# A weight load moved from behind the first norm of an attention stage to behind its key cast

## The chip, the cores and the metric

The kernel runs on one core of one Trainium2 chip. The metric is the device time of one execution in microseconds (us). PE is the matrix engine, PEld its weight loads, DVE the vector engine, ACT the scalar engine, POOL the GpSimd engine and SP the SyncE engine, which here only issues DMAs. DMAs are issued by SP (hardware queue, q1 in the profile) and by POOL (software queue, q0), and both queues are served by the core's 16 DMA engines.

## The reference

Inputs are q, k, v of shape (8 batches, 8 heads, 576 tokens, 64), two spectral weights `w_r` and `w_i` of 64 modes x 512 x 512, and `w_ch` of 512 x 512, all fp32. First comes causal attention in a window of 128 tokens with a linear distance bias per head, then a Fourier mixing layer on its output.

```python
scores = scale * q @ k.T;  rel = i - j
scores = where((rel >= 0) & (rel < 128), scores - slope[h] * abs(rel), -1e9)
x = softmax(scores) @ v                     # heads side by side: (8, 576, 512)
X = rfft(x, axis=1)[:, :64]                 # 64 modes
Yr = Xr @ w_r - Xi @ w_i;  Yi = Xr @ w_i + Xi @ w_r      # one 512x512 matrix per mode
u = x + irfft(Y, n=576, axis=1)
out = u + relu(u @ w_ch)
```

The 128 matrices of `w_r` and `w_i` are 1 MB each in fp32. They are the bulk of what has to be read.

## The kernel before

**Attention.** The work is cut into 16 units, one for each batch and half of the heads (four heads). A unit has a fixed list of steps: three casts from fp32 to bf16 on DVE (`cast` of q and k at L241, of v at L236 and L238), transposes of q and k on PE with an evacuation each (L253, L259), four score tiles (`score`, L287), four exponentials on ACT (`exp`, L297), two multiplications by the decay table (`mask`, L308), two value products (`value`, L334), and two norms (`norm`: a reciprocal at L349 and a multiplication at L350 that writes x). At the end of each second unit come the forward Fourier products (`spectrum`, L371) and their evacuation (`channels`, L392).

**The order of the work** is written out by hand. `STAGE` (L38 to L44) lists the steps of one pipeline stage with a lag for each; the loop at L544 runs the list once for each stage, and a step of lag l works on unit `stage - l`. So the key cast (lag -2) of a stage is that of unit `stage + 2`, the query cast (lag -3) that of unit `stage + 3`, and the two norms (lag 1) are those of unit `stage - 1`. On DVE the order within a stage is: cast of v, cast of k, first norm, cast of q, the two masks, second norm. Each engine executes its instructions in the order in which they are written; engines wait for each other by semaphores.

**Loads of q, k and v.** Each cast issues, on SP, the load of the unit two further on into the buffer that it has just read (L243): one DMA of 576 KB for q or k, and five for v (four of 128 KB, one of 64 KB). There are two buffers for each of q, k and v. SP issues them in order, and each of its DMAs also waits for the DMA eight before it on SP.

**Weights.** `load_w` (L453) issues one weight matrix on POOL: 1 MB of fp32 is read and 512 KB of bf16 is written, cast on the way. One tile is issued ahead of the loop (L516), one in each of the stages 1 to 13 (`AHEAD`, L418) into the pool `early`, and seven more (`LATER`, L419) at the ends of stages 12 to 15 into q, k and v buffers that are no longer needed. So that the weight of a stage is not issued at once, POOL first copies one element that the first norm of the stage has written (L556):

```python
if stage in AHEAD:
    if stage:
        b, g = at.units[stage - 1]
        nc.gpsimd.tensor_copy(gate[:1, :1], x[:1, b, 0, 256 * g : 256 * g + 1])
    load_w(AHEAD[stage], early)
```

The copy has no other use. POOL does nothing else in these stages, so it stands at the copy until the norm is done and then issues the weight.

**After attention.** The other weights follow in the order of use, into pools whose buffers come free when attention ends and later when PE has used an earlier tile (`load_packs`, L465, two matrices at a time). PE multiplies the spectra of all batches by each matrix (L861). Between these products come inverse Fourier products, the projection by `w_ch` and the transposes that they need. After the last matrix the last four modes are patched in, and the output is computed and stored (L784 to L830).

Of the kernel before, what the change touches and what calls it, by code (L numbers as in the profile page):

```python
# [71 lines left out]
def _forward_table(nc, pool, F, S):  # L72


    NM = F.shape[2] // 2
    tok = pool.tile([P, FULL + 1], I32)
    nc.gpsimd.iota(tok[:, :FULL], [[P, FULL]], base=0, channel_multiplier=1)
    for bb in range(2):
        nc.gpsimd.iota(
            tok[64 * bb : 64 * bb + 64, FULL : FULL + 1], [[0, 1]],  # L80
            base=FULL * P, channel_multiplier=1,
        )
    mode = pool.tile([P, NM], I32)
    nc.gpsimd.iota(mode, [[1, NM]], base=0, channel_multiplier=0)
    prod = pool.tile([P, FULL + 1, NM], FP32)
    nc.vector.tensor_tensor(
        out=prod,
        in0=tok.unsqueeze(-1).broadcast_to([P, FULL + 1, NM]),
        in1=mode.unsqueeze(1).broadcast_to([P, FULL + 1, NM]),
        op=ALU.mult,  # L90
    )
    turn = pool.tile([P, FULL + 1, NM, 2], FP32)
    for ri in range(2):
        nc.vector.tensor_scalar(turn[:, :, :, ri], prod, float(S) / (4 - 2 * ri), 1.0 / S,
                                op0=ALU.add, op1=ALU.mult)
    whole = pool.tile([P, FULL + 1, NM, 2], FP32)
    nc.vector.tensor_scalar(whole, turn, MAGIC, MAGIC, op0=ALU.add, op1=ALU.subtract)
    nc.vector.tensor_tensor(out=turn, in0=turn, in1=whole, op=ALU.subtract)
    nc.scalar.activation(F[:, : FULL + 1].rearrange("p a b -> p (a b)"),
                         turn.rearrange("p a b c -> p (a b c)"), AF.Sin, scale=TWO_PI)  # L100
    yield
    nc.gpsimd.memset(F[:64, FULL + 1], 0.0)
    nc.gpsimd.tensor_copy(F[64:, FULL + 1], F[64:, FULL])
    nc.gpsimd.memset(F[64:, FULL], 0.0)
# [298 lines left out]
def kernel(  # L403
# [10 lines left out]
    nc = tc.nc  # L414
# [9 lines left out]
    x = const.tile([P, B, FULL + 1, DM], BF16, name="x")  # L424
# [4 lines left out]
    gate = const.tile([P, 8], BF16, name="gate")  # L429
# [23 lines left out]
    def load_w(n, pool, chosen=None):  # L453

        for i in ([i for i in todo_w if i not in again][:n] if chosen is None else chosen):
            todo_w.remove(i)
            src = (moe_w_r, moe_w_i)[i % 2][i // 2].rearrange("(p a) e -> p a e", a=4)
            homes[i] = pool
            t = spare.pop(0) if pool is None else pool.tile([P, 4, DM], BF16, tag="w", name="w")
            for part in ((slice(0, 4),) if i < 2 * NM - 1  # L460
                         else (slice(0, 2), slice(2, 3), slice(3, 4))):
                nc.gpsimd.dma_start(out=t[:, part], in_=src[:, part])
            wq[i] = [t[:, a] for a in range(4)]
# [27 lines left out]
    with ExitStack() as actx:  # L491
        at = _Attention(tc, actx, q, k, v, (ident, F, FT), x, XC, raw)
        n = len(at.units)
        for w, u in (("q", 0), ("k", 0), ("q", 1), ("k", 1), ("v", 0), ("v", 1)):
            at.load(w, u)
        done = set()

        def run(name, arg, u):
            if 0 <= u < n and (name, arg, u) not in done:
                done.add((name, arg, u))  # L500
                getattr(at, name)(u, arg)

        make_identity(nc, ident)
        pool = _Scratch(x[:, B - 2 :].rearrange("p b t c -> p (b t c)").bitcast(FP32))
        wt = at.ps.tile([P, P], FP32, tag="av", bufs=1, name="warm")
        for _ in range(24):
            nc.tensor.matmul(wt, lhsT=ident, rhs=ident, start=True, stop=True)
        table = _forward_table(nc, pool, F, S)
        next(table)
        nc.vector.memset(norm, 2.0 / S)  # L510
        nc.vector.memset(norm[:32], 1.0 / S)
        for t in at.qkT:
            nc.vector.memset(t[:, 1, :, S:], 0.0)
        at.distances(pool)
        at.fixtures(0)
        load_w(1, early)  # L516
        next(table, None)
        at.fixtures(1)
        nc.gpsimd.memset(XC[:, 4 * NC * NM :], 0.0)
        run("cast", "q", 0)  # L520
        run("transpose", "q", 0)
        run("cast", "k", 0)
        run("transpose", "k", 0)
        run("evacuate", "q", 0)
        for h in (1, 3):
            at.decay(h)
        run("evacuate", "k", 0)
        run("score", 1, 0)
        for h in (0, 2, 1, 3):
            at.offset(h)  # L530
        run("cast", "q", 1)
        run("transpose", "q", 1)
        run("evacuate", "q", 1)
        run("score", 0, 0)
        run("exp", 1, 0)
        for h in (0, 2):
            at.decay(h)
        run("exp", 0, 0)
        run("cast", "k", 1)
        run("cast", "v", 0)  # L540
        side = {0: [(at.offset, 4), (at.offset, 6), (at.decay, 5), (at.offset, 5), (at.decay, 7),
                    (at.offset, 7), (at.decay, 4), (at.decay, 6)]}
        lags = [lag for _, _, lag in STAGE]
        for stage in range(min(lags), n + max(lags)):  # L544
            for name, arg, lag in STAGE:
                run(name, arg, stage - lag)
                if name in ("transpose", "exp") and side.get(stage):
                    for _ in range(1 + (name == "transpose")):
                        fn, h = side[stage].pop(0)
                        fn(h)  # L550
            if stage == 3:
                at.inverse_table()
            if stage in AHEAD:
                if stage:
                    b, g = at.units[stage - 1]
                    nc.gpsimd.tensor_copy(gate[:1, :1], x[:1, b, 0, 256 * g : 256 * g + 1])  # L556
                load_w(AHEAD[stage], early)
            if stage in LATER:
                load_w(LATER[stage], None)

    with ExitStack() as mctx:
# [273 lines left out]
        for g in range(NM // 4):  # L835
# [5 lines left out]
            for i in range(8):  # L841
                k = 8 * g + i
# [159 lines left out]
```

## Time and profile before

| | us |
|---|---|
| median of 3 runs | 439.54 |
| lowest, highest | 439.48, 439.64 |
| span of the profiled execution | 439.4 |
| first and last gate copy (L556) start | 28.0, 118.3 |
| last attention exponential on ACT ends | 133.1 |
| weight products of PE (L861) | 140.8 to 405.7 |

| engine | busy us | share of the span |
|---|---|---|
| PE | 320.6 | 73% |
| DVE | 183.7 | 42% |
| ACT | 162.1 | 37% |
| POOL | 87.0 | 20% |

The profile is one execution, taken by the hardware profiler; its span runs from the first instruction to the last. The shares of busy time are means over parts that have different limits: attention up to about 140 us, the stream of weights up to about 405 us, and the output. In the rows of a timeline, the first number is the start, the second the duration (for several instructions from the first start to the last end), and the brackets give the idle time of the engine before it and what ended that. In a table of stretches the DMA share is the mean busy share of the 16 DMA engines; packets of two queues on one engine can overlap in the records, so that it goes somewhat over 1. GB/s counts bytes as written, so a weight counts with its 512 KB of bf16.

### The profile page before, as it was taken

What the parts mean: (1) busy time and instruction counts of PE and PEld (TensorE: products, weight loads), DVE (VectorE), ACT (ScalarE), POOL (GpSimd) and SP (SyncE); (2) the same over time, 40 slices, a digit from 0 to 9 for tenths busy, and PEclk for the clock granted to TensorE, in tenths of its full rate; (3) what the DMA queues carried; (4) which work ended last, traced back from release to release, by engine and by line L of the source; (5) the groups of instructions that cost most, each with busy time, mean ns of one, the idle gap of its engine ahead of it and who ended that gap; (6) DMA issues with size and microseconds to landing.
All of it is one profiled execution on the core that took longest, in us unless ns stands there. A gap on an engine that the chain in (4) does not pass through costs nothing. (4 is left out here: it accounts for less than half of the span.)

```text
span 439.4 us, 8314 instructions
## 1 busy us (share of the span) xinstructions
PE 320.6 (73%) x3509; PEld 177.6 (40%) x3509; DVE 183.7 (42%) x332; ACT 162.1 (37%) x211; POOL 87.0 (20%) x162
## 2 busy tenths in 40 slices
PE   4679899969796724553443387999889999698982
PEld 3357577647665411111111133444444444233430
DVE  7689699788783301010000022332222232122684
ACT  6769799987781000000000012323232323101780
POOL 8611011100323101322113111111111110012500
PEclk8679899999999965555555569999999999989997
DMA  8999999999999999999999999999999999997598
GB/s 280 306 329 301 300 292 312 266 302 283 266 224 213 216 214 213 214 213 214 214 213 215 214 214 214 214 215 215 214 214 215 216 213 214 214 215 135 199 368 306
DMA packets 52489, 105.54 MB, mean 240 GB/s; under 512 B 4052, under 2 KB 23396, under 8 KB 52452
## 3 DMA queue, kind: packets, MB, share of 16 engines
q0 software_dynamic: 18992, 67.22, 76.5%
q1 hardware_dynamic: 33460, 37.79, 26.3%
q8 instruction: 27, 0.44, 0.4%
q14 instruction: 10, 0.08, 0.0%
HBM read 162.53 MB, written 9.44 MB: 391 GB/s over the span
## 5 line engine op out<-in xcount | busy, mean ns | idle before, releaser
L861 PE MATMUL acc<-w,XC 128*32 128x512 bf16 x456 | 80.8, 485 | 68.8 <-DMA w<-in_moe_w_i_dram 35.4
L861 PEld LDWEIGHTS <-XC 128*32 128x32 bf16 x508 | 38.7, 148 | 110.1 <-issue 85.0
L297 ACT ACTIVATE att<-sc 128x1024 bf16<-128x1024 f32 x64 | 64.0, 1031 | 10.0 <-PE sc L287 10.0
L627 ACT CAST ZW<-zw 128x512 bf16<-128x512 f32 x8 | 4.7, 586 | 144.7 <-PE zw L625 144.7
L334 PE MATMUL av<-vb,att 128*128 128x132 bf16 (+1 forms) x576 | 38.4, 217 | 11.6 <-DVE x L350 8.8
L599 DVE TENSOR_SCALAR yq<-acc 128x512 bf16<-128x512 f32 x14 | 9.6, 687 | 82.2 <-PE acc L861 82.2
L334 PEld LDWEIGHTS <-att 128*128 128x128 bf16 x704 | 36.6, 98 | 17.2 <-DVE x L350 13.0
L693 PE MATMUL my<-wch,xT 128*64 128x512 bf16 x288 | 34.5, 381 | 5.8 <-ACT x L724 4.3
L702 ACT CAST XW<-my 128x512 bf16<-128x512 f32 x36 | 19.3, 589 | 50.5 <-PE my L650 50.5
L674 DVE COPY xT<-tr 128x1024 bf16<-128x1024 bf16 x18 | 12.5, 692 | 55.0 <-PE tr L672 55.0
L259 ACT COPY qkT<-tp 128x1152 bf16<-128x1152 bf16 x30 | 33.5, 1115 | 5.3 <-PE tp L253 4.5
L481 POOL DMA_DIRECT2D w<-in_moe_w_i_dram x23 | 16.3, 710 | 66.9 <-PE acc L861 44.2
L481 POOL DMA_DIRECT2D w<-in_moe_w_r_dram x22 | 15.6, 709 | 68.5 <-PE acc L861 48.1
L287 PE MATMUL sc<-qkT 64*64 64x256 bf16 (+2 forms) x640 | 25.7, 269 | 2.5 <-ACT qkT L259 1.6
L350 DVE TENSOR_TENSOR x<-av,rec 128x640 bf16<-128x640 f32 x32 | 26.4, 825 | 1.1
L693 PEld LDWEIGHTS <-xT 128*64 128x64 bf16 x288 | 17.1, 109 | 21.6 <-issue 9.2
L817 DVE TENSOR_TENSOR o<-yy,r 128x1024 f32<-128x1024 f32 (+1 forms) x22 | 21.5, 1025 | 4.8 <-DMA Z<-yq 2.6
L236 DVE CAST vb<-vr 64x1024 bf16<-64x1024 f32 x32 | 22.7, 708 | 0.4 <-DMA vr<-in_v_dram 0.2
L287 PEld LDWEIGHTS <-qkT 64*64 64x64 bf16 x640 | 14.8, 110 | 19.8 <-issue 16.5
L556 POOL COPY gate<-x 1x1 bf16<-1x1 bf16 x13 | 5.5, 423 | 86.2 <-DVE x L350 86.2
L724 ACT CAST x<-my 128x512 bf16<-128x512 f32 x18 | 10.6, 586 | 31.0 <-PE my L650 31.0
L274 PE MATMUL sc<-bias,ident 128*128 128x512 bf16 x64 | 20.7, 408 | 1.1 <-ACT att L297 1.1
(134 smaller groups left out, 431.0 us busy)
## 6 DMA issues: line engine op xcount, KB each, us to landing
w<-in_moe_w_i_dram POOLq DMA_DIRECT2D x23, 1024.0 KB, 35.8
w<-in_moe_w_r_dram POOLq DMA_DIRECT2D x22, 1024.0 KB, 35.7
qr<-in_q_dram SPq DMA_DIRECT2D x16, 576.0 KB, 9.2
kr<-in_k_dram SPq DMA_DIRECT2D x16, 576.0 KB, 8.2
vr<-in_v_dram SPq DMA_DIRECT2D x64, 128.0 KB, 7.6
w<-in_moe_w_r_dram POOLq DMA_DIRECT2D x16, 512.0 KB, 14.3
w<-in_moe_w_i_dram POOLq DMA_DIRECT2D x13, 512.0 KB, 24.0
out_dram<-o SPq DMA_DIRECT2D x13, 512.0 KB, 4.6
```

The costliest lines, as they stand in the source:

```text
L236: nc.vector.tensor_copy(self.vb[u % 2][row, :, :, :, W * half : W * half + D], src[row, :2])
L259: (self.nc.vector.tensor_copy if u < 2 and w == "q" else self.nc.scalar.copy)(dst.rearrange("q h (p j) -> q h p j", j=TPP), tp.rearrange(" ...
L274: nc.tensor.matmul(sc[:, e], lhsT=self.ident, rhs=self.bias[:, hv].rearrange("p j n -> p (j n)"), start=True, stop=False, skip_group_check ...
L287: nc.tensor.matmul(sc[64 * half : 64 * half + 64, e, j * 256 + c0 : j * 256 + c0 + n], lhsT=qkT[row, 1, h, k0 + j : k0 + P : 2], rhs=qkT[r ...
L297: self.nc.scalar.activation(self.att[u % 2][:, kt * 8 * P : (kt + 1) * 8 * P], sc.rearrange("p e n -> p (e n)"), AF.Exp, scale=1.0 / math. ...
L334: nc.tensor.matmul(bank[:, qt * W : qt * W + rhs[j].shape[1]], lhsT=att[:, o : o + P], rhs=rhs[j], start=(n == 0 and j == 0), stop=(n == l ...
L350: nc.vector.tensor_tensor(out=self.x[:, b, :, cs].rearrange("p t (h d) -> p h t d", h=2), in0=tiles[:, :, :, :D], in1=rec.unsqueeze(-1).br ...
L481: nc.gpsimd.dma_start(out=t.rearrange("p s a e -> p s (a e)"), in_=w[kinds.pop()][m : m + 2].rearrange("m (p a) e -> p m (a e)", a=4))
L693: nc.tensor.matmul(mm[ROWS[half]], lhsT=lhsT, rhs=wch[:, dt], start=(dt == 0), stop=False, skip_group_check=True,)
L702: nc.scalar.copy(XW[:, j, n], mms[n])
L817: nc.vector.tensor_tensor(out=o[:, c], in0=yy[:, c], in1=r[:, c], op=ALU.add)
L861: nc.tensor.matmul(into[32 * (m % 4) : 32 * (m % 4) + 32], lhsT=XC[:, c0 : c0 + 31 * NM + 1 : NM], rhs=wq[t][a], start=(ri == 0 and a == 0 ...
```

## The change

The element that POOL copies ahead of the weight of a stage is no longer one of x, written by the first norm of unit `stage - 1`, but one of the bf16 key tile, written by the key cast of unit `stage + 2` in the same stage. On DVE that cast stands just ahead of the first norm.

```diff
             if stage in AHEAD:
-                if stage:
-                    b, g = at.units[stage - 1]
-                    nc.gpsimd.tensor_copy(gate[:1, :1], x[:1, b, 0, 256 * g : 256 * g + 1])
+                nc.gpsimd.tensor_copy(gate[:1, :1], at.casted[stage + 2, "k"][:1, 0, 0, :1])
                 load_w(AHEAD[stage], early)
```

The order of the instructions is the same on each engine. The copies are 13 before and 13 after. As POOL now reads the key tile, of which there are two, the key cast that writes the same buffer two stages later waits for POOL too (eleven casts); three casts into x of the later part (L725) no longer wait for POOL.

## The prediction

> **What bounds the kernel now.** I read the page's 40 slices first, then the chain of work that ended last, then stretches of one attention stage each, then the GpSimd (POOL) timeline and the waits of the DMA-issuing queues.
>
> The slices and the queue table of the page:
>
> ```profile
> PE   4679899969796724553443387999889999698982
> ACT  6769799987781000000000012323232323101780
> DMA  8999999999999999999999999999999999997598
> ...
> q0 software_dynamic: 18992, 67.22, 76.5%
> q1 hardware_dynamic: 33460, 37.79, 26.3%
> ```
>
> The DMA engines are full from the second slice (11 us) to about 400 us, while PE and ACT have long empty stretches in between. The two queues together are worth 102.8% of 16 engines over the span. Queue 0 carries the weights (issued by POOL, cast on the way), queue 1 the loads of q, k, v and the output.
>
> The end of the PE timeline, where the last weights are used (start, duration, line, count, and the idle time before):
>
> ```profile
> 397.80 1.02 PE L861 MATMUL pa<-w,XC 128*32 128x512 bf16 x4 [0.58 <-DMA w<-in_moe_w_r_dram]
> 400.24 1.02 PE L861 MATMUL pa<-w,XC 128*32 128x512 bf16 x4 [0.22 <-DMA w<-in_moe_w_i_dram]
> 405.27 0.38 PE L861 MATMUL acc<-w,XC 128*32 128x512 bf16 x1 [0.19 <-DMA w<-in_moe_w_i_dram]
> ```
>
> PE waits for the last pieces of weight, so 405.3 us is set by the weight stream. The chain of the page covers only what follows (from 406.3 us), and that tail of 439.4 - 405.3 = 34.1 us has no weight load in it. So the time is the end of the weight stream plus a fixed tail, and an edit in the attention stages counts only by what it does to that stream.
>
> Now the stages. Stretches from one weight issue to the next; the columns are length, busy time (instructions) of PE, PEld, DVE, ACT and POOL, then granted clock, DMA share, GB/s:
>
> ```profile
> 59.30:66.50 7.20, 6.81 (x126) 5.11 (x126) 6.59 (x13) 6.70 (x8) 1.16 (x4) 1.00 1.02 278
> 79.50:86.70 7.20, 6.34 (x114) 5.13 (x112) 6.48 (x12) 6.47 (x9) 0.89 (x2) 1.00 1.05 292
> 118.70:130.40 11.70, 10.79 (x198) 8.42 (x196) 9.24 (x18) 9.91 (x12) 3.73 (x9) 1.00 1.10 238
> 130.40:140.00 9.60, 6.46 (x120) 5.17 (x118) 4.87 (x11) 3.25 (x6) 4.60 (x8) 1.00 1.06 213
> ```
>
> PE, DVE and ACT are at about nine tenths in a stage, and yet the DMA share is at or above 1.02 in every one of the 15 stretches that I asked for between 21 and 140 us. The last stretch is weights alone (213 GB/s). From about 122 us on, the stream does not break before 400 us: rates of 213 to 216 GB/s in nearly all later slices.
>
> **The change, step by step.** It removes 13 one-element POOL copies that read the first norm's output and puts 13 in their place that read the key cast of the same stage; nothing else moves in any engine's order. The weight DMA is the next instruction on POOL, so what moves is its issue.
>
> 1. How far. The POOL and DVE timelines of one stage:
>
> ```profile
> 77.21 0.76 DVE L241 CAST k<-kr 128x1152 bf16<-128x1152 f32 x1
> 77.88 0.21 DVE L349 RECIPROCAL rec<-av 128x10 f32<-128x10 f32 x1
> 78.13 0.82 DVE L350 TENSOR_TENSOR x<-av,rec 128x640 bf16<-128x640 f32 x1
> ...
> 79.09 0.18 POOL L556 COPY gate<-x 1x1 bf16<-1x1 bf16 x1 [6.12 <-DVE x L350]
> 79.54 0.71 POOL L462 DMA_DIRECT2D w<-in_moe_w_r_dram  x1 [0.27 <-issue]
> ```
>
> The key cast ends at 77.97, the norm at 78.95. The issue moves forward by 1.0 to 1.1 us (reciprocal 0.21 plus multiply 0.82 plus gaps). In one stage the norm waits 1.49 us for PE, and there it is 2.6 us (cast end 47.58, gate 50.29). Where the gate copy took 0.57 rather than 0.18 us, it ran beside the query cast; it would now run beside the norm, so up to 0.4 us more may come. I take 1.1 to 1.5 us in twelve stages and some 3 us in one.
>
> 2. What that does to the stream. Each tile is 512 KB, 524,288 B / 214 GB/s = 2.45 us of all DMA engines, now and after. No byte is added, none goes. With the engines full, an earlier start puts a weight in front of loads that then finish later by the same engine time; the end of all the work stays. Term: 0 us, exact only as far as the engines are full. How far they are not, bounds the term. In 1 us slices between 20 and 121 us the DMA share is under 1.00 in twelve; the deficits add up to 0.52 us, the largest a slice at 0.76 (61 to 62 us). A second way: q and k of a unit are 1.18 MB at the 393 GB/s of the slices 26 to 28 us, 3.0 us; v is 0.59 MB at the 306 GB/s of 28.5 to 31 us (1100 of its 1205 packets are under 2 KB), 1.9 us; with the weight, 7.4 us per stage. The gates lie (118.3 - 28.0) / 12 = 7.5 us apart, so 12 x 0.12 = 1.5 us is the most that better packing could save. I take -0.1 us, close to nothing, because the dips lie on both sides of a weight transfer, and a shift fills one and opens another.
>
> 3. What the moved weight displaces. Twelve of the stages have loads of v, k and q under way. Their consumers: DVE waited 7.4 us in all for q (6 times, longest 2.1), 0.3 for k, 0.2 for v. A later q lengthens that stage's compute, but compute is not the bound there: the next stages' loads are already queued. Term: 0; without that cover, up to 1.1 us once, not per stage, since the shift is the same in each stage.
>
> 4. The end of attention. After 118.7 us, weights are queued back to back; five single tiles (2.45 us each) are issued by 123.5 us, and POOL then waits:
>
> ```profile
> 123.47 0.54 POOL L462 DMA_DIRECT2D vr<-in_moe_w_i_dram  x1 [2.64 <-DMA vr<-in_v_dram]
> 129.35 1.06 POOL L462 DMA_DIRECT2D vr<-in_moe_w_r_dram  x2 [5.34 <-DVE vb L236]
> ```
>
> The pair at 129.35 waits for the last v cast. Its tiles land 9.0 and more (median 10.3) us after issue; the quickest landing of a tile in the stages was 6.6 us. So about 3.7 us pass before a late pair leaves the DMA engines empty. The last v load lands within the 0.6 us after 127.4 us (4 packets of queue 1 there, none later), and its cast runs at 128.97: 1.5 us of slack ahead of that. The last v load may be 5 us later before the stream breaks. Term: 0.
>
> 5. The new waits. Eleven key casts now also wait for the POOL copy that read the buffer two stages before, which ran some 11 us or more earlier; three late casts lose a POOL wait. A semaphore instruction on DVE took 21 to 50 ns: under 0.6 us in all, beside full DMA engines. Behind a key cast on DVE stand the norm and the query cast; they would be late only if POOL were a stage late, and POOL is idle 4.9 to 9.2 us ahead of each gate. Term: 0.
>
> Sum: 439.4 (span) - 0.1 = 439.3 us; the three runs give 439.48 to 439.64, about 0.1 above the span, so **439.4 us**. About 0.2% (0.9 us) is what a measurement of this kernel can tell from no change.
>
> **The rivals.**
>
> *Better packing (faster).* The weight falls into the dips ahead of its present start, the one at 61 us first. For: that dip stands ahead of a weight whose issue (59.3 us) had gone out 2 us before. Against: most dips are 0.05 us or less. If two thirds to all of the 1.5 us go: 438.0 to 438.5, middle 438.4 us.
>
> *The loads run dry (slower).* SyncE's loads wait each for the eighth DMA before it:
>
> ```profile
> SPq L211 <- DMA qr<-in_q_dram: 17.1, 12, 2.3
> SPq L211 <- DVE vt L238: 15.9, 9, 2.9
> ```
>
> Twelve times a v load could not be issued until a query load had landed. If a weight that starts earlier delays those landings, the next v, k and q loads are issued later, and once the weight is through, the engines have too little queued. It decides from the point where queue 1 is empty when a weight ends. Price: a dip like that of 61 us (0.24 us) in each of 13 stages is 3.1 us, in half of them 1.6 us: 441.0 us. Against: after a weight the share is back at 1.0 within a slice in nearly every stage.
>
> [...]
>
> *The last v load is starved (slower).* The same, only at the end of attention: more than 5 us late, then microsecond for microsecond. About 441 us.
>
> *Nothing moves on the DMA engines,* since a weight waits behind what is queued: no packets of a weight move in the 2.5 us after the issue at 28.5 us. It gives 439.5 us, inside the forecast.
>
> **How the numbers follow.** Forecast, with the case that nothing moves: 0.62 (own range 438.7 to 440.3). Better packing 0.18. Loads running dry 0.16, starved v 0.04. So faster by over 0.2% 0.18, within 0.62, slower 0.20. The range goes from 438.3 (most of the packing gain) to 441.2 (half the dips, and a little): it leaves out about 0.15.
>
> **What would show it.** Right: the gate copies end 1 to 1.5 us sooner after the key cast, the weights land sooner by as much, the stretch 118 to 140 us is still at a share of 1.05, and the last weight lands within 0.5 us of before, with a tail of 34.1 us. Wrong: a sum of deficits between 20 and 121 us that differs from 0.52 by a microsecond; DVE waits for q, k or v well above 7.9 us together with DMA shares under 1; a break in the weight stream near 134 us; or a tail of other length, for instance by another granted clock after 405 us (1.00 in each slice from 400 to 414 us now).

## The result and the profile after

| | us |
|---|---|
| changed kernel, median of 22 runs (lowest to highest) | 443.07 (439.2 to 445.12) |
| kernel before, median of 22 runs beside them | 439.65 (438.66 to 443.01) |
| ratio, 95% interval | 1.0057 (1.0038 to 1.0075) |
| span of the profiled execution after; its own time | 441.2; 442.94 |

The change makes the kernel slower, by 0.4 to 0.8%. The forecast was no change. Both kernels spread over several us, which three runs of before (439.48 to 439.64) had not shown. The ratio is that of the mean times of the executions in the fast state (here 442.57 to 440.08 us, all of them), so it need not be that of the medians.

The slices of the page after, to be laid beside those of before:

```profile
PE   5589899979865664354333377989889999689982
ACT  6849899978860000000000012232222322102780
DMA  8999999999996999999999999999999999998598
GB/s 284 319 317 308 292 318 294 320 289 305 245 201 126 214 215 213 214 214 214 214 211 215 214 214 215 215 215 214 214 214 215 215 213 214 214 215 157 190 378 302
```

The thirteenth slice (132 to 143 us) has a hole that the profile of before does not have, called the break from here on: DMA 6 instead of 9, 126 GB/s instead of 213. The same place in stretches of 6 us (columns as in the prediction: length, busy PE, PEld, DVE, ACT, POOL, clock, DMA share, GB/s), first before, then after:

```profile
124.00:130.00 6.00, 5.49 (x108) 4.54 (x103) 5.03 (x10) 4.80 (x6) 0.66 (x3) 1.00 1.06 214
130.00:136.00 6.00, 4.83 (x95) 3.67 (x93) 3.15 (x7) 2.81 (x4) 3.50 (x6) 1.00 1.06 214
136.00:142.00 6.00, 3.28 (x40) 2.30 (x38) 2.57 (x6) 0.55 (x2) 1.50 (x3) 0.90 1.07 216
```

```profile
124.00:130.00 6.00, 4.59 (x88) 3.15 (x79) 0.88 (x2) 4.97 (x7) 0.00 (x0) 1.00 1.07 217
130.00:136.00 6.00, 0.00 (x0) 0.00 (x0) 2.47 (x5) 0.28 (x1) 0.87 (x2) 0.66 0.30 61
136.00:142.00 6.00, 4.49 (x52) 4.34 (x53) 2.66 (x6) 0.00 (x0) 3.89 (x7) 0.50 0.94 173
```

From 130 to 136 us PE does nothing and the DMA engines are at 0.30. The 1.06 of before is the weights' queue almost alone (queue 0 has 106.2% of the engines from 136 to 142 us there), so a share over 1 needs no overlap of two queues. Measured against it, the last two stretches lack (1.06 - 0.30) x 6 + (1.06 - 0.94) x 6 = 5.3 us of DMA time. Who waits there, on DVE first: the v casts of the last two units, before and then after:

```profile
121.79 1.39 DVE L236 CAST vb<-vr 64x1024 bf16<-64x1024 f32 x2 [0.23 <-DMA vr<-in_v_dram]
...
127.67 1.38 DVE L236 CAST vb<-vr 64x1024 bf16<-64x1024 f32 x2
```

```profile
119.16 1.39 DVE L236 CAST vb<-vr 64x1024 bf16<-64x1024 f32 x2 [0.43 <-DMA vr<-in_v_dram]
...
133.45 1.39 DVE L236 CAST vb<-vr 64x1024 bf16<-64x1024 f32 x2 [8.53 <-DMA vr<-in_v_dram]
```

Then POOL, after:

```profile
114.44 0.18 POOL L554 COPY gate<-k 1x1 bf16<-1x1 bf16 x1 [5.64 <-DVE rec L349]
114.89 0.53 POOL L462 DMA_DIRECT2D w<-in_moe_w_i_dram  x1 [0.27 <-issue]
...
116.45 0.56 POOL L462 DMA_DIRECT2D kr<-in_moe_w_i_dram  x1
120.84 0.53 POOL L462 DMA_DIRECT2D vr<-in_moe_w_i_dram  x1 [3.83 <-DVE vb L236]
135.13 1.05 POOL L462 DMA_DIRECT2D vr<-in_moe_w_r_dram  x2 [13.76 <-DVE vb L236]
```

The v cast of the last unit waits 8.5 us for its load, where it did not wait before. The last 64 KB of that load, issued at 118.4 us, are the row below (the last number is us from issue to landing); before, the same 64 KB took 7.0 us:

```profile
vr<-in_v_dram SPq DMA_DIRECT2D x1, 64.0 KB, 15.1
```

POOL stands behind that cast, since the next two weights go into v's buffer, and cannot issue anything for 13.8 us. What was queued runs out from 131 us on. This is the mechanism that the prediction had named "the last v load is starved", with a chance of 0.04.

### The profile page after: what moved, and what is told of

Same layout as the page of the kernel before. It is cut to its first block, busy times and chain, and to the rows that moved or that the text cites. A ratio compares the mean times of both kernels' runs of the same rounds, so it can differ in the third digit from the quotient of the medians.

```text
span 441.2 us, 8318 instructions
## 1 busy us (share of the span) xinstructions
PE 323.0 (73%) x3509; PEld 181.6 (41%) x3509; DVE 184.9 (42%) x332; ACT 162.1 (37%) x211; POOL 84.5 (19%) x162
## 5 line engine op out<-in xcount | busy, mean ns | idle before, releaser
L859 PE MATMUL acc<-w,XC 128*32 128x512 bf16 x456 | 78.8, 479 | 64.9 <-DMA w<-in_moe_w_i_dram 32.7
L334 PE MATMUL av<-vb,att 128*128 128x132 bf16 (+1 forms) x576 | 41.0, 225 | 17.5 <-DVE x L350 12.0
L334 PEld LDWEIGHTS <-att 128*128 128x128 bf16 x704 | 39.2, 103 | 22.9 <-DVE x L350 16.5
L815 DVE TENSOR_TENSOR o<-yy,r 128x1024 f32<-128x1024 f32 (+1 forms) x22 | 21.6, 1025 | 4.3 <-DMA Z<-yq 2.6
L723 DVE CAST x<-my 128x512 bf16<-128x512 f32 x18 | 12.5, 692 | 21.3 <-PE my L648 21.3
```

The lines of the kernel that those rows point to most:

```text
L334: nc.tensor.matmul(bank[:, qt * W : qt * W + rhs[j].shape[1]], lhsT=att[:, o : o + P], rhs=rhs[j], start=(n == 0 and j == 0), stop=(n == l ...
L815: nc.vector.tensor_tensor(out=o[:, c], in0=yy[:, c], in1=r[:, c], op=ALU.add)
L859: nc.tensor.matmul(into[32 * (m % 4) : 32 * (m % 4) + 32], lhsT=XC[:, c0 : c0 + 31 * NM + 1 : NM], rhs=wq[t][a], start=(ri == 0 and a == 0 ...
```

## The experiments

The theory after this profile: the loss is all in stage 13, whose four weight tiles begin an unbroken queue of weights while the last v loads are still on their way. Its rivals: the thirteen earlier weights hurt the loads in all the stages; the new wait for the key tile costs; a gain in the stages is hidden under the loss. Medians are of all runs of a kernel, beside runs of before on the same chip; in the last column stand the executions above 442.5 us. That line is a rough one: e12_after_again, at 442.48 us, has the break.

| kernel | median us | ratio to before (95%) | above 442.5 us |
|---|---|---|---|
| before, four batches | 439.65, 440.04, 439.84, 440.0 | | 16 of 85 |
| after | 443.07 | 1.0057 (1.0038 to 1.0075) | 12 of 22 |
| e1_only13 | 444.98 | 1.0081 (1.0035 to 1.0126) | 6 of 6 |
| e2_first12 | 439.75 | 0.9975 (0.9923 to 1.0028) | 1 of 6 |
| e3_v15pool | 438.73 | 0.9949 (0.9905 to 0.9994) | 0 of 6 |
| e4_hold13 | 440.2 | 0.9989 (0.9938 to 1.0041) | 1 of 6 |
| e5_old_v15pool | 438.86 | 0.9972 (0.9948 to 0.9996) | 0 of 12 |
| e6_v14v15pool | 439.93 | 0.9996 (0.9971 to 1.0022) | 0 of 12 |
| e8_early13 | 446.36 | 1.0122 (1.0081 to 1.0163) | 6 of 6 |
| e9_pool_new | 439.44 | 0.9973 (0.9944 to 1.0001) | 0 of 12 |
| e10_pool_old | 439.19 | 0.9974 (0.9946 to 1.0003) | 0 of 12 |
| e11_widev | 439.78 | 1.0005 (0.9968 to 1.0042) | 2 of 12 |

### The change in stage 13 alone, and in the other twelve alone

On the kernel before (e1_only13; e2_first12 has `stage < 13` in place of `stage == 13`):

```diff
-                if stage:
+                if stage == 13:
+                    nc.gpsimd.tensor_copy(gate[:1, :1], at.casted[stage + 2, "k"][:1, 0, 0, :1])
+                else:
                     b, g = at.units[stage - 1]
                     nc.gpsimd.tensor_copy(gate[:1, :1], x[:1, b, 0, 256 * g : 256 * g + 1])
```

> Only stage 13 has the new gate, stages 1 to 12 the old one. Theory (the last 64 to 256 KB of v are starved once the weights are queued without a break; the engines then run empty until POOL gets past the last v cast): DVE waits several us for the last v, a break in the DMA share between 126 and 138 us worth 2 to 5 us, no gain ahead of it: 441 to 445 us. Rival (the loss comes from what all thirteen earlier weights do to the loads in the stages): no break, 439.5 to 440 us.

> Stages 1 to 12 have the new gate, stage 13 the old one. Theory (starved last v load, set by the weights of stages 12 and 13): the break is gone or much smaller, and what the stages gain stays, 437.0 to 439.5 us. Rival (loss in all the stages): 442 to 443 us as with the whole change.

Measured: 444.98 us with the one stage, 439.75 us with the other twelve. The stretches of e1_only13:

```profile
124.00:130.00 6.00, 0.00 (x0) 0.00 (x0) 2.30 (x5) 1.87 (x2) 0.53 (x1) 0.67 1.06 217
130.00:136.00 6.00, 5.22 (x61) 4.62 (x62) 3.33 (x6) 1.94 (x2) 0.00 (x0) 0.50 0.61 126
136.00:142.00 6.00, 4.68 (x86) 3.67 (x85) 4.46 (x9) 2.81 (x4) 2.99 (x5) 0.98 0.59 102
```

One moved gate makes the whole break: 0.61 and 0.59 where before has 1.06 and 1.07, 5.6 us of DMA time, a little more than expected. It is not the last v load that is late first, as had been expected, but that of the unit before. The v casts of the last two units in e1_only13:

```profile
126.37 1.39 DVE L236 CAST vb<-vr 64x1024 bf16<-64x1024 f32 x2 [6.38 <-DMA vr<-in_v_dram]
...
135.46 1.39 DVE L236 CAST vb<-vr 64x1024 bf16<-64x1024 f32 x2 [1.58 <-DMA vr<-in_v_dram]
```

POOL needs both casts before it can issue its next weights, so either load can make the break when it is late. The twelve others give no difference that the interval can tell from none, and the gain in the stages that was expected of them (437.0 to 439.5 us) did not show. The rival "loss in all the stages" is out. Why the one gate alone is above 442.5 us in all 6 executions, and the whole change in 12 of 22, was not settled.

### An even earlier gate in stage 13

```diff
-                if stage:
+                if stage == 13:
+                    nc.gpsimd.tensor_copy(gate[:1, :1], at.vb[1][:1, 0, 0, 0, :1])
+                else:
                     b, g = at.units[stage - 1]
```

> The kernel before, with only the gate of stage 13 moved, behind the v cast of that stage, some 3 us ahead of the old place and 0.7 us ahead of the key cast's end. Theory (starved v load): at least as slow as with the gate of stage 13 at the key cast, 444 to 447 us, with a break of 3 to 6 us. Rival (the wait for the key tile itself costs, not the moment of issue): no break, 439.5 to 440 us.

Measured: 446.36 us; DVE waited 10.3 us for v, all of it for that of the unit before the last, and the DMA share was 0.50 and 0.49 from 130 to 142 us, a break of some 6.8 us, more than expected. No engine waits for a key tile here, so the new wait is not the cause; the moment of issue is. The three places of this gate in order of time, v cast, key cast, norm, give 446.4, 445.0 and 439.8 us (the median of all 85 runs of before). The intervals of the first two overlap; both lie clear of the third.

### The last v load in the weights' queue

```diff
+            q = nc.gpsimd if u == 15 else nc.sync
             for h in range(4):
-                nc.sync.dma_start(
+                q.dma_start(
                     out=t[:, :2, h],
...
-            nc.sync.dma_start(
+            q.dma_start(
                 out=t[64:96, 2],
```

> The whole change, but the five loads of v of the last unit are issued by POOL into the queue of the weights, ahead of the weights of stage 13; they are plain copies of the same bytes. Theory (two queues take turns and the short packets of v lose): the last v lands within about 5 us of its issue, DVE does not wait over 1 us for it, no break in the DMA share before 140 us, 436.5 to 439.5 us. Rival (POOL's order or the wait for the casts makes the break, not the taking of turns): DVE still waits over 3 us for v, 442 to 444 us.

Measured: 438.73 us. The five loads now stand in POOL's queue ahead of the weights of stage 13. The DMA share stays at 1.06 to 1.08 from 118 to 142 us, and the last v cast does not wait. DVE still waited 2.6 us for v, but for that of the unit before, which SP issues, and the DMA share did not fall for it. The same bytes and the same weights, without the break, as expected. POOL still waits for the last v casts before its last weights, and with the load in time that wait makes no break, so the rival is out. But the run moves something else too. POOL needs 3.7 us to issue the five loads, so the first weight of stage 13 goes out 5.5 us behind the start of that stage's v cast, where it is 3.1 us after and 4.1 us before. The order in the queue and the later weight act together here; this run does not part them, and e4_hold13 below has the later weight alone.

> The whole change, with the v loads of the last two units issued by POOL. Theory (with v of the last unit alone on POOL, DVE still waited 2.6 us for v of the unit before, but no DMA engine was empty, so nothing is lost): the same as with one unit, 438 to 439.5 us. Rival (that wait still costs): 1 us less, 437 to 438 us.

```diff
-            q = nc.gpsimd if u == 15 else nc.sync
+            q = nc.gpsimd if u >= 14 else nc.sync
```

Now the unit before goes through POOL as well: 439.93 us, no break, and no gain. It lies somewhat above the expected range; why it is not as quick as with one unit was not settled.

### Holding the weights of stage 13 back

```diff
-                    nc.gpsimd.tensor_copy(gate[:1, :1], at.casted[stage + 2, "k"][:1, 0, 0, :1])
+                if stage < 13:
+                    nc.gpsimd.tensor_copy(gate[:1, :1], at.casted[stage + 2, "k"][:1, 0, 0, :1])
+                else:
+                    b, g = at.units[stage - 1]
+                    nc.gpsimd.tensor_copy(gate[:1, :1], x[:1, b, 0, 256 * g + 128 : 256 * g + 129])
```

> The new gate in stages 1 to 12; in stage 13 the weight and the three behind it wait for the second norm of the stage, some 6 us behind the key cast. Theory (starved last v load): v of the last unit lands ahead of those weights, DVE waits under 0.5 us for it, no break in the DMA share, 436.5 to 439 us. Rival (weights held back leave the engines empty): a DMA share under 0.9 between 108 and 122 us, 440 to 442 us.

Measured: 440.2 us; both theories were half right. The stretches of e4_hold13:

```profile
118.00:124.00 6.00, 5.46 (x104) 4.06 (x103) 4.84 (x9) 5.22 (x6) 3.43 (x6) 1.00 0.79 161
124.00:130.00 6.00, 5.34 (x105) 4.09 (x99) 4.84 (x9) 4.98 (x7) 1.80 (x3) 1.00 1.05 211
130.00:136.00 6.00, 3.65 (x73) 3.35 (x71) 3.41 (x7) 0.37 (x1) 2.87 (x5) 1.00 1.08 218
```

The first weight of stage 13 goes out 7.5 us behind the start of the v cast. The break at 130 us is gone and DVE waits 0.7 us for v, but the engines now run short ahead of it: 0.79 from 118 to 124 us, (1.06 - 0.79) x 6 = 1.6 us. So a later weight alone takes the break away too, at a price. Between too early and too late there are only a few us.

### The kernel before and the change, a second time

> The kernel before, unchanged, for a second profile. If its own spread (438.8 to 445.9 us in the last runs) is the same starved load in some executions, then the time and the break go together: about 439.5 us with the DMA share at 1.05 from 124 to 142 us, or 443 us and more with DVE waiting over 4 us for v and a break. If the spread comes from elsewhere (granted clock, tail), a time of 443 us would go with an unbroken DMA share.

> The whole change, unchanged, for a second profile. If time and break go together, a run of 439 to 440 us has a DMA share of 1.0 and more from 124 to 142 us, and one of 443 us and more has DVE waiting over 6 us for v and the share under 0.8 in part of that stretch.

Both are unchanged copies. The change gave 442.48 us, between the two cases that were expected, with 7.8 us of waiting for v and a share of 0.46 from 130 to 136 us, as in the second. The kernel before gave 443.96 us, and its profile has the break as well:

```profile
124.00:130.00 6.00, 5.22 (x96) 3.63 (x92) 1.31 (x3) 4.89 (x8) 0.00 (x0) 1.00 1.07 216
130.00:136.00 6.00, 0.00 (x0) 0.00 (x0) 1.42 (x3) 0.81 (x1) 0.00 (x0) 0.65 0.41 82
136.00:142.00 6.00, 3.37 (x39) 3.22 (x40) 3.58 (x7) 0.00 (x0) 3.63 (x6) 0.50 0.75 136
```

Lacking DMA time: (1.06 - 0.41) x 6 + (1.06 - 0.75) x 6 = 5.8 us. Its span (442.1 us) lies 5.8 and 5.0 us above those of the same kernel with v on POOL (436.3 us in e10_pool_old, 437.1 us in e5_old_v15pool). So the break is no new thing; the change moves a gate that already stood at the edge, and 12 of 22 executions lie above 442.5 us instead of 16 of 85: it makes the break more frequent. That those are the ones with the break is shown for the profiled ones alone: every profile with a time above 442 us has it, and none below 440 us has one of more than 1 us at that place.

### Is there a gain in the stages?

> The kernel before, all gates at the first norm, with the five v loads of the last unit issued by POOL ahead of the weights of stage 13. Theory A (the earlier weight brings the stages nothing; all that the change does is the starved v load): no break in the DMA share, and the same time as with the new gates and v on POOL, 438 to 439.5 us; key casts of stages 1 to 13 some 88 us apart, as in the runs with the new gate. Theory B (the earlier weight speeds the stages by 1 to 2 us and the starved load takes back more): 439.5 to 441 us, the key casts 89.5 to 90.5 us apart.

> The whole change with the v loads of the last unit issued by POOL, again, beside the next one. Theory A (the earlier weight brings the stages nothing once the starved load is out of the way): within 0.2% of the next one, both 438 to 439.5 us. Theory B (it brings 1 us or more): 1 us or more faster than the next one.

> The kernel before with the v loads of the last unit issued by POOL, again, beside the one ahead. Theory A: within 0.2% of it. Theory B: 1 us or more slower than it. In both, no run at 443 us or above, as no load is starved.

These have the edit of e3_v15pool, e9_pool_new on the changed kernel and the two others on the kernel before. With v of the last unit on POOL, the copies at the gate of stage 13 no longer wait for anything, so in effect these kernels differ in the gates of stages 1 to 12 alone. Old gates: 438.86 and 439.19 us; new gates: 438.73 and 439.44 us. The means of all runs are 439.24 us (24 runs) and 439.29 us (18). The time from the key cast of stage 1 to that of stage 13 on DVE, in one profile each: 87.6 to 90.3 us with old gates (six profiles, mean 88.6), 87.2 to 90.1 us with new ones (eight, mean 88.3). No gain is shown: the means differ by 0.05 us, with a standard error of some 0.26 us.

### Larger packets for the last v load

```diff
+                if u == 15:
+                    flat = t.rearrange("p s h d -> p (s h d)")
+                    nc.sync.dma_start(
+                        out=flat[:, 256 * h : 256 * h + 256],
+                        in_=sv[h, : FULL * P].rearrange("(p j) d -> p (j d)", j=4),
+                    )
+                    continue
                 nc.sync.dma_start(
                     out=t[:, :2, h],
```

> The whole change; the four large v loads of the last unit take four tokens in a row per partition, so that a packet is 1024 B instead of 512 B and there are half as many; the rows go to other places, so unit 15 computes with permuted v. The last 64 KB stay as they were. Theory (one packet of each queue in turn beside the weights): the load moves twice the bytes per turn, and what is left of it when the weights become unbroken takes half the time; DVE waits 0 to 4 us for v, 438.5 to 441 us, no run over 443. Rival (a fixed share of bytes beside the weights): DVE waits 6 to 9 us, 442 to 444 us as with the whole change.

Measured: 439.78 us, DVE waited 1.8 us in its profile, 2 of 12 executions were above 442.5 us, where none above 443 us had been expected and two were (443.04 and 443.96). With half as many packets most executions are without the loss, and a few still seem to have it. The counts of packets fit that. Packets, MB and share of each queue, after, from 121 to 127 us:

```profile
q0 software_dynamic: 315, 1.16, 95.1%
q1 hardware_dynamic: 311, 0.15, 12.2%
```

Then e11_widev from 121 to 124 us:

```profile
q0 software_dynamic: 151, 0.55, 90.8%
q1 hardware_dynamic: 107, 0.11, 12.9%
```

After, the two queues move the same number of packets, one for one: 4 KB of weight against 512 B of v (without some packets of 4 B that both counts hold, 282 to 289), which leaves the loads 0.15 MB in 6 us, 25 GB/s. In the prediction's stretch without weights a like load moved at 306 GB/s. In e11_widev 107 packets, nearly all of 1 KB, are 0.11 MB in half that time. The counts agree with a taking of turns between the queues, packet by packet: 315 to 311 here, 154 to 153 in e11_widev from 124 to 127 us. How a DMA engine chooses between them, no run here shows.

The kernel before with the break (e7_before_again), from 124 to 130 us:

```profile
q0 software_dynamic: 350, 1.26, 104.9%
...
q1 hardware_dynamic: 20, 0.01, 0.8%
```

350 weight packets are 22 for each of the 16 DMA engines, and the loads move 20: about what one engine gets through, one for one, if the other fifteen are done with v. The cast did not start before the last packets of queue 1 had moved (16 of them from 130 to 134 us, the cast at 134.57 us). That one engine was behind is an inference from the counts; why it was, is open.

## Why the prediction was wrong

**What bounds the kernel: right.** PE takes the last weight at 407.1 us after, again straight behind its DMA. The tail, counted as in the prediction from the start of that product, is 441.2 - 407.1 = 34.1 us, as before:

```profile
407.14 0.38 PE L859 MATMUL acc<-w,XC 128*32 128x512 bf16 x1 [0.19 <-DMA w<-in_moe_w_i_dram]
```

**Step 1, the issue moves by 1.0 to 1.5 us: right at the lower end.** In the stage that the prediction showed, the weight's issue stands 0.6 us behind the key cast's end (76.89 to 77.48) where it stood 1.6 us behind it: 1.0 us. All gate copies take 0.18 us, as expected beside the norm; the 0.4 us that this saves hardly moves the issue, since the DMA instruction starts 0.4 to 0.6 us behind the copy's start in 12 of the 13 copies of before and in 11 of 13 after.

**Steps 2 and 3, nothing in the stages: right.** e2_first12, and the two pairs with v on POOL, show no difference. A gain or loss of a few tenths of a us stays possible. Neither "better packing" nor "the loads run dry" was seen at the size that the prediction gave them: the share from 60 to 118 us is 1.08 after and 1.06 before.

**Step 4, the end of attention: this is the step that failed.** It said that the last v load may be 5 us later before the stream breaks, put that at 0, and gave the rival a chance of 0.04 and about 441 us. The break is 5.3 us in the profile after. The slack was about right: in e2_first12 DVE waited 2.2 and 1.2 us for the last v, and only (1.06 - 0.98) x 6 = 0.5 us of DMA time were lost from 136 to 142 us. What was wrong is how late the load can be. I took the shift of the weights, 1.1 us, as the size of the delay. But once the queue of weights had no gap, the loads that were still queued got one short packet for each weight packet (311 to 315 in 6 us after), 25 GB/s where a like load had 306 GB/s without weights beside it. By these two rates, what is left at that moment takes some twelve times as long: when the weights reached 0.97 of the engines (from 119 us on after, from 122 us on before), the loads still had some 550 packets to move after and some 290 before. The last v cast started 21.6 us behind the v cast of stage 13 after, 13.0 us before. The shift of 1 us is not needed for that, since in e7_before_again it was 22.3 us with the old gate; the shift makes it frequent. The trace of before showed the sign. The last 64 KB of v, issued at 121.0 us, took 7.0 us to land (first row), and from 123 to 126 us the weights had 99.5% of the engines and the loads 6.1%:

```profile
vr<-in_v_dram SPq DMA_DIRECT2D x1, 64.0 KB, 7.0
```

```profile
q0 software_dynamic: 164, 0.60, 99.5%
q1 hardware_dynamic: 75, 0.04, 6.1%
```

I read the slack from it as a fixed margin, and did not ask what it is made of.

**Step 5, the new waits: right.** e8_early13 has none of them and is slow as well.

**Span and median.** The prediction set the span (439.4 us) 0.1 us below the runs. In the later profiled executions the time is 1.7 to 2.1 us above the span (442.94 to 441.2 after). If that holds for the first profile too, it is of an execution of about 441 us, without a break, whose stages took long (90.3 us between those key casts, 87.7 us in e10_pool_old). This is also most of the reason why the two spans lie only 1.8 us apart with a break of 5.3 us in one: the profile of before reached the key cast of stage 13 at 116.39 us, that of after at 113.55 us. That the span of this execution lies so near the three times is luck; the prediction took the one for the other. And three runs that agree to 0.16 us hid that about one execution in five of the kernel before (16 of 85) is above 442.5 us. Had the range been built on that spread, it would have been wider.

**A better version.** The kernel before with the last v load on POOL (e5_old_v15pool and e10_pool_old) has no break in its two profiles, and the slowest of its 24 runs is at 441.25 us. By its two ratios it is 0.26 to 0.28% faster than before, but the intervals are 0.9948 to 0.9996 and 0.9946 to 1.0003, so the gain in the mean is only just to be told from none. Clearer is that the executions above 442.5 us are gone: 0 of 24, 16 of 85 before.

## What to carry to other kernels

Where two queues feed the same DMA engines, ask at each point whether the one with the large packets becomes gapless: from then on a load of short packets that is still under way can take much longer (25 instead of 306 GB/s here, with 512 B against 4 KB), and a transfer that others stand behind should be out by then or go into the same queue ahead. A margin read from one trace is only worth as much as the rate it was read at; work out what is left to move, and at which rate, when the order changes. And if a wait sits at the edge of covering, look at the spread of many runs, not at the median of three.

## What the runs showed of the hardware

- Beside weights without a gap, the two DMA queues moved packets one for one in these stretches, though of unlike size: 315 of the weights (4 KB) and 311 of the loads (512 B) from 121 to 127 us after, 154 (0.57 MB) and 153 (0.09 MB) from 124 to 127 us in e11_widev. With fewer loads left it was 166 to 64 (127 to 130 us after), and in e7_before_again 350 to 20 (124 to 130 us), about what one engine alone would give.
- A one-element copy on POOL took 0.57 to 0.64 us beside a cast on DVE that reads fp32 and writes bf16 in on-chip memory (seven gate copies of before), 0.51 us beside the multiplication by the decay table (one), and 0.18 us with DVE idle (the other five) or beside the norm, which reads the accumulators (after).
- PE's granted clock fell to 0.66 and 0.50 in the break (130 to 142 us), in which PE had nothing to do at first; no cost of it was seen: PE still waited for the last weight at 407.1 us.
